# Batch 1's casts and copies reordered, H2's weight sums moved, and the last stores merged, in a linear-attention and gated-MLP kernel

## The chip, the cores and the metric

The kernel runs on one core of a Trainium2 chip. The metric is device time in microseconds (us) of one execution. A core has TensorE (PE, matrix products, with its weight loads shown as PEld), VectorE (DVE), ScalarE (ACT), GpSimd (POOL) and SyncE (SP). Each has its own instruction queue, worked through in order; between queues only semaphores set an order. DMAs are issued from the queues of SP, ACT and POOL and are carried out by 16 DMA engines.

## The reference

The inputs q, k and v are (8 batches, 8 heads, 576 positions, 64) in float32; w_in is 512x2048, w_out 2048x512, beta 2048.

```python
def phi(x): return np.where(x > 0, x, np.exp(x) - 1.0) + 1.0
q_p, k_p = phi(q), phi(k)
kv  = einsum('bhsd,bhse->bhde', k_p, v)
z   = k_p.sum(axis=2)
num = einsum('bhsd,bhde->bhse', q_p, kv)
den = einsum('bhsd,bhd->bhs', q_p, z)[..., None] + 1e-06
x   = (num / den), heads side by side: (4608 tokens, 512)
h   = x @ w_in
g   = h / (1 + exp(-beta * h))
out = g @ w_out                       # (4608, 512), float32
```

## The kernel before

**Tiling.** The work goes batch by batch. A batch has 576 positions, that is 64 groups (g) of 9 (j). Positions j = 0 to 7 make four token tiles of 128 rows, which are the batch's 512 columns in the MLP; the positions j = 8 of all eight batches are gathered in `xT_tail` and make a ninth block of 512 columns at the end (b = 8, called B in the code). The MLP of block b has an H phase (`h_phase`: 16 groups `ff` of four matmuls of 512 columns, L404, each followed by a silu on ACT, L412) and a Y phase (`y_phase` for blocks 0 and 1; `y_fast`, L755, for blocks 2 to 8, which saves products by sums and differences of g and of w_out, the latter prepared in `ws` by `w_sum`, L697). Below, H1 is the H phase of block 1, Y2 the Y phase of block 2, and so on.

**Overlap.** While TensorE works on the MLP of block b, the attention of batch b+1 is done between its groups: `kv_both` (L213; k^T v and, through a column of ones, z), then the numerators (`numer`, or `numer_all`, L319, from batch 2 on), the division on DVE into `xs_sb`, and the transpose into `xT`, on TensorE for batches 0 and 1 (`x_trans`, L381, with a copy by ACT or DVE), by DMA from batch 2 on. phi is an exp on ACT (`phi_exp`), a relu on DVE (`phi_relu`, L168) and a minimum on DVE (`phi_min`, L175). v arrives in float32 in the one buffer `vf` and is cast into `vaug` by POOL (`v_copy`, L203); only when both halves are cast may the next batch's v be loaded into `vf` (`load_v`).

**Order.** It is written out by hand (`manual_schedule`): each engine executes its instructions in the order in which the Python issues them. Up to L690 that is a straight list; afterwards `h_phase` and the Y phases call what `at(sh, ff, ...)` and `at(sy, n, ...)` hang behind a group or a product. The pool `hps` has four PSUM banks (`bank`), used in a ring by h, y and part of the numerators; `wps` has two pairs of banks (`banks`), used in a ring by `kv_both`, numerators and x transposes.

**Places that the change touches.** Batch 1's stretch is L627 to L690: MLP products `y_mm(0, t, i)` of block 0 (token tile t, quarter i of w_out) stand between `kv_both(1)`, `numer(1, t)` and `x_trans(1, t)`. `y_out` copies a finished y from PSUM with DVE and `y_store` sends it from SP. `w_out_scale(nc.scalar, 3)` scales quarter 3 of w_out on ACT. In `next_loads` (L842), called behind H's first group, POOL casts the next batch's v, waits by the tiny copy into `gate` for the transposed q of that batch (`qTd`) and then issues the loads of the batch after it. Two calls per store are due to `half(i)`: 64 partitions each. `g_diff` and `g_sums` (L716, L720) are DVE work on g behind groups 3, 7, 11 and 15 of an H phase.

Of the kernel before, what the change touches and what calls it, by code (L numbers as in the profile page):

```python
# [16 lines left out]
def kernel(  # L17
# [183 lines left out]
            phi_min(b, a, pr)  # L201

    def v_copy(eng, b, pr):  # L203
        eng.tensor_copy(  # L204
            vaug[b % 2][:, pr, :, :, 0:D],
            vf[:, 2 * pr : 2 * pr + 2].rearrange("p h j d -> p j h d"),
        )

    def half(hh):
        return slice(hh * G, (hh + 1) * G)  # L210
# [47 lines left out]
    def q_copy(eng, b, pr, tp):  # L258
        copy(eng, st[b, "qT"][:, pr, 0:4].rearrange("p t h n -> p (t h n)"), tp)
# [166 lines left out]
    def rows(b, ts):  # L426
# [2 lines left out]
            return out[b * S : (b + 1) * S, :].rearrange("(g j) m -> g j m", j=J)[:, ts]  # L429
        return out.rearrange("(b g j) m -> g b j m", b=B, j=J)[:, ts, J - 1]  # L430

    def y_store(b, t, c0=0, c1=512):
        for i in range(2):
            nc.sync.dma_start(
                out=rows(b, slice(2 * t + i, 2 * t + i + 1))[:, 0, c0:c1],
                in_=(y1, y2)[t % 2][half(i), (t // 2) % 2, c0:c1],
            )
# [6 lines left out]
    def w_out_scale(eng, i, cs=range(4)):  # L444
        for c in cs:
            ff = 4 * i + c
            if eng is nc.scalar:
                eng.mul(w_out_sb[i][:, c, :], w_out_f[i][:, c, :], rbeta[:, ff : ff + 1])
            else:
                eng.tensor_scalar(  # L450
                    w_out_sb[i][:, c, :], w_out_f[i][:, c, :], rbeta[:, ff : ff + 1],
                    1.0, ALU.mult, ALU.mult,
                )
# [6 lines left out]
    def load_v(b):  # L460
        if b < B:
            load(nc.gpsimd, vf, v, b)
# [169 lines left out]
            phi_relu(1, x, pr, xin(1, x, pr))  # L632
    phi_min(1, "q", 0)
    phi_min(1, "q", 1)
    for pr in range(2):
        v_copy(nc.gpsimd, 1, pr)
    load_v(2)
    for i in range(2):
        for t in range(4 - i):
            y_mm(0, t, i, yps[t])  # L640
# [4 lines left out]
    q_last(1, qtp[1][:, 1024 : 1024 + 2 * P])  # L645
    y_mm(0, 3, 1, yps[3])
    q_copy(nc.scalar, 1, 0, qtp[0][:, 0:1024])
    w_out_scale(nc.vector, 2)
    phi_min(1, "k", 0)
    phi_min(1, "k", 1)  # L650
    q_copy(nc.vector, 1, 1, qtp[1][:, 0:1024])
    q_copy_last(nc.vector, 1, qtp[1][:, 1024 : 1024 + 2 * P])
    w_out_scale(nc.scalar, 3)
    for t in range(3):
        y_mm(0, t, 2, yps[t])
    kv_both(1)
    phi_tile(2, "q")
    phi_tile(2, "k")
    y_mm(0, 3, 2, yps[3])
    numer(1, 0)  # L660
    y_mm(0, 0, 3, yps[0])
    numer(1, 1)
    x_trans(1, 0, nc.scalar)
    phi_exp(2, "q", 0, xin(2, "q", 0))
    y_mm(0, 1, 3, yps[1])
    numer(1, 2)
    y_out(0, 0, yps[0])
    x_trans(1, 1, nc.scalar)
    phi_exp(2, "q", 1, xin(2, "q", 1))
    y_mm(0, 2, 3, yps[2])  # L670
    numer(1, 3)
    y_out(0, 1, yps[1])
    x_trans(1, 2, nc.scalar)
    phi_exp(2, "k", 0, xin(2, "k", 0))
    y_mm(0, 3, 3, yps[3])
    x_trans(1, 3, nc.vector)
    phi_exp(2, "k", 1, xin(2, "k", 1))
    table(ACTF.Silu)
    y_out(0, 2, yps[2], store=False)
    y_out(0, 3, yps[3], store=False)  # L680
    numer_mm(1, 4)
    for pr in range(2):
        phi_relu(2, "q", pr, xin(2, "q", pr))
        phi_min(2, "q", pr)
    q_trans_dma(2)
    numer_xs(1, 4)
    x_trans_dma(1, 4)
    for t in range(2, 4):
# [36 lines left out]

    def h_phase(b, x, side):
        for ff in range(FC):
            hp = bank("h_ps")
            h_mm(x, ff, hp)
            silu(b, ff, hp)  # L730
            if b in FAST:
                if ff in (3, 7):
                    g_diff(b, slice(ff - 3, ff + 1))
                if ff in (11, 15):
                    g_sums(b, ff - 11, ff - 7)
            run(side, ff)
# [18 lines left out]
    def y_fast(b, side):  # L755

        g = g_sb[b % 2]
        pa, pd, pc, pb = [bank(n) for n in ("ya", "yd", "yc", "yb")]

        pbs = [banks("yb")[:, 0], banks("yb")[:, 0]] if b == B else [pb, pb]  # L760

        def part(n0, half2):
            def lhs(c, p):
                t0 = half2 * HM + p * P
                return g[:, n0 + c, t0 : t0 + P]
            return lhs

        def sums(n):
            return lambda c, p: gs[n][:, c, p * P : (p + 1) * P]

        def plain(n0, c0):
            return lambda c: w_out_sb[(n0 + c) // 4][:, (n0 + c) % 4, c0 : c0 + HM]

        def wsum(n):
            return lambda c: ws[n][:, c, :]

        def product(ps, lhs, rhs, first, ts=range(2), apart=False):
            for p in ts:
                for c in range(8):
                    nc.tensor.matmul(  # L780
                        ps[:, p * HM : (p + 1) * HM], lhs(c, p), rhs(c),
                        start=(first and (p == 0 or apart) and c == 0), stop=True,
                        skip_group_check=True,
                    )

        def v3(ps):
            return ps.rearrange("p (a m) -> p a m", a=2)

        r1 = work.tile([P, 512], F32, tag="r1", name="r1", bufs=1)
        u2 = work.tile([P, 512], F32, tag="u2", name="u2", bufs=1)  # L790
        u4 = work.tile([P, 512], F32, tag="u4", name="u4", bufs=1)
        u3 = work.tile([P, 512], F32, tag="u3", name="u3", bufs=1)
        if b < B - 2:
            table(ACTF.Exp)
        product(pa, part(0, 0), plain(0, 0), True)
        nc.scalar.copy(r1, pa)
        run(side, 0)
        product(pd, sums(2), wsum(2), True)
        run(side, 1)
        product(pa, part(8, 0), plain(8, 0), False)  # L800
        nc.scalar.copy(y1[:, :, 0:HM], v3(pa))
        run(side, 2)
        product(pc, sums(1), wsum(1), True)
        nc.vector.tensor_add(u2, pc, r1)  # L804
        nc.vector.tensor_add(u3, pd, u2)  # L805
        run(side, 3)
        if b == B:
            for i in range(2):
                nc.sync.dma_start(
                    out=rows(b, slice(i, i + 3, 2))[:, :, 0:HM], in_=y1[half(i), :, 0:HM]  # L810
                )
        for p in range(2):
            product(pbs[p], sums(0), wsum(0), True, (p,), b == B)
        for p in range(2) if b == B else ():
            ps = slice(p * HM, (p + 1) * HM)
            nc.vector.tensor_add(y2[:, p, HM:DM], pbs[p][:, ps], u3[:, ps])
        if b < B:
            nc.vector.tensor_add(y2[:, :, HM:DM], v3(pb), v3(u3))  # L818
        run(side, 4)
        product(pd, part(8, 1), wsum(3), False)  # L820
        nc.vector.tensor_add(y2[:, :, 0:HM], v3(pd), v3(u2))
        for i in range(2):
            nc.sync.dma_start(out=rows(b, slice(4 + i, 4 + i + 3, 2)), in_=y2[half(i)])
        run(side, 5)
        if b < B:
            product(pb, sums(3), plain(8, HM), False)
            nc.vector.tensor_add(y1[:, :, HM:DM], v3(pb), v3(u2))
            for i in range(2):
                nc.sync.dma_start(out=rows(b, slice(i, i + 3, 2)), in_=y1[half(i)])
        else:  # L830
            for p in range(2):
                ps = slice(p * HM, (p + 1) * HM)
                product(pbs[p], sums(3), plain(8, HM), False, (p,))
                nc.vector.tensor_add(y1[:, p, HM:DM], pbs[p][:, ps], u2[:, ps])  # L834
                for i, eng in enumerate((nc.sync, nc.scalar)):
                    eng.dma_start(
                        out=rows(b, slice(i + 2 * p, i + 2 * p + 1))[:, 0, HM:DM],
                        in_=y1[half(i), p, HM:DM],
                    )
        run(side, 6)  # L840

    def next_loads(b):  # L842
# [8 lines left out]
    for b in range(1, B + 1):  # L851
        n, m = b + 1, b + 2
        sh, sy = {}, {}
        if n < B:
            at(sh, 0, lambda: next_loads(n))
            at(sh, 8 if b == 1 else 1, lambda: kv_both(n))
            at(sh, 11 if b == 1 else 4, lambda: numer_all(n))
        if b in (1, 2) and FAST:
            for k_ in ((0, 2), (1, 3))[b - 1]:
                for n_ in range(2):  # L860
                    at(sh, 15 if b == 1 else k_, lambda k_=k_, n_=n_: w_sum(k_, n_))
        if m < B:
            y = (lambda a, f: f) if b in FAST else (lambda a, f: a)
            at(sy, 0, lambda: phi_tile(m, "q"), lambda: phi_part(m, "q", 0))
            at(sy, 1, lambda: phi_part(m, "q", 1))
            at(sy, 1, lambda: q_trans_dma(m))
            at(sy, y(6, 3), lambda: phi_tile(m, "k"), lambda: phi_part(m, "k", 0))
            at(sy, y(8, 4), lambda: phi_part(m, "k", 1), lambda: table(ACTF.Silu))
        h_phase(b, xT[b % 2] if b < B else xT_tail, sh)
        (y_fast if b in FAST else y_phase)(b, sy)  # L870
# [30 lines left out]
```

## Time and profile before

| | us |
|---|---|
| median of 3 runs | 282.42 |
| the runs | 280.89, 282.42, 282.59 |
| profiled execution | 280.67 |
| its span | 278.9 |
| TensorE busy in the span | 267.2 (96%) |
| DVE busy | 169.2 (61%) |
| ACT busy | 169.1 (61%) |
| POOL busy | 46.3 (17%) |

The span runs from the first to the last instruction in the trace; the execution's own time has some 1.8 us around it. The stretches of the span: batch 0's attention up to about 21 us, H0 to 32, Y0 with batch 1's attention to 51.6, H1 to 67, Y1 to 81, H2 to 97, Y2 to 109.7, and then some 28 us for each further block; the last product ends at 273.7. A line of a timeline gives the start (us), the busy time, engine, source line, operation, output and inputs with sizes, and in brackets the idle time of the engine before it and what ended it. A busy matmul includes its way through the pipeline: matmuls that follow one another are nearer in their starts than their busy time. DMA calls appear under SPq, ACTq or POOLq with the time their issue takes.

### The profile page before, as it was taken

The page shows a single profiled execution, that of the slowest core. Times are in us where ns is not written, and L with a number is a line of the kernel's source. Part 1 is how long each engine was busy: PE and PEld are TensorE (multiplying, and loading weights), DVE is VectorE, ACT ScalarE, POOL GpSimd, SP SyncE. Part 2 cuts the span into 40 slices and gives each one's busy share as a digit, 9 for nine tenths or more (in the row PEclk, how much of TensorE's full clock was granted, in tenths as well). Part 3 has the DMA queues.
Part 4 walks back from the last instruction along what each step waited for, and adds up shares of the span by engine and source line. Part 5 has one row for each costly group of instructions (what it writes and reads, how often), then busy time and mean ns, then how long its engine had stood idle before and what let it go on. Part 6 is the DMA issues. An engine that isn't in the chain of part 4 may idle for free.

```text
span 278.9 us, 6374 instructions
## 1 busy us (share of the span) xinstructions
PE 267.2 (96%) x2689; PEld 167.0 (60%) x2697; DVE 169.2 (61%) x329; ACT 169.1 (61%) x231; POOL 46.3 (17%) x60
## 2 busy tenths in 40 slices
PE   6799999999999999999999999999999999999992
PEld 2475455445444487548754875487548745864681
DVE  4772485958848797568757885788572414321532
ACT  4838876975925794579457945794572076127500
POOL 5923012303043030304030303030000000000000
PEclk9999999999999999999999999999999999999998
DMA  7999999559999946994799659956430130041014
GB/s 237 248 207 351 268 373 264 142 94 180 289 150 182 300 65 101 205 293 66 105 198 284 79 97 204 280 83 98 142 75 12 35 118 0 0 101 52 0 40 113
DMA packets 49292, 42.76 MB, mean 153 GB/s; under 512 B 30816, under 2 KB 41072, under 8 KB 49264
## 3 DMA queue, kind: packets, MB, share of 16 engines
q0 software_dynamic: 13040, 23.40, 36.0%
q1 hardware_dynamic: 36032, 18.82, 33.1%
q8 instruction: 21, 0.34, 0.5%
q10 hardware_dynamic: 192, 0.14, 0.2%
q14 instruction: 7, 0.06, 0.1%
HBM read 36.71 MB, written 9.44 MB: 165 GB/s over the span
## 4 chain that ended last, share of the span: by engine, by line
PE 59%; DVE 2%; issue 0%; DVEq 0%
PE h_ps L404 30%; PE yb L780 8%; PE yd L780 8%; PE ya L780 8%; PE yc L780 4%; PE kvp L223 1%; PE nps L331 1%; DVE phi_q L175 1%; DVE r L168 0%; DVE u L804 0%; DVE y L818 0%; DVE u L805 0%; DVE y L834 0%; DVE phi_k L175 0%; DVEq L818 0%
## 5 line engine op out<-in xcount | busy, mean ns | idle before, releaser
L412 ACT ACTIVATE g<-h_ps,beta_c 128x512 bf16<-128x512 f32 x144 | 97.8, 688 | 68.7 <-PE h_ps L404 68.7
L404 PE MATMUL h_ps<-xT,w_in 128*128 128x512 bf16 (+1 forms) x560 | 114.8, 361 | 0.4 <-DVE xT L241 0.2
L404 PEld LDWEIGHTS <-w_in 128*128 128x128 bf16 x624 | 57.3, 98 | 63.1 <-DVE xs_sb L346 1.1
L780 PEld LDWEIGHTS <-stage 128*128 128x128 bf16 x448 | 43.8, 98 | 5.5 <-issue 0.4
L780 PEld LDWEIGHTS <-g 128*128 128x128 bf16 x336 | 32.9, 98 | 5.4
L204 POOL CAST vaug<-vf 128x1152 bf16<-128x1152 f32 x14 | 18.8, 1372 | 83.8 <-DMA vf<-in_v_dram 83.8
L419 PE MATMUL y_ps<-w_out,g 128*128 128x512 bf16 x123 | 28.7, 379 | 0.4 <-issue 0.2
L780 PE MATMUL ya<-w_out,g 128*128 128x256 bf16 x224 | 26.7, 273 | 0.0
L718 DVE TENSOR_TENSOR stage<-g 128x1024 bf16<-128x1024 bf16 x14 | 9.6, 685 | 21.6 <-ACT g L412 21.6
L722 DVE TENSOR_TENSOR stage<-g 128x1024 bf16<-128x1024 bf16 x14 | 9.7, 692 | 20.7 <-ACT g L412 20.7
L346 DVE TENSOR_TENSOR xs_sb<-nps,rden 128x448 bf16<-128x448 f32 (+3 forms) x30 | 20.7, 689 | 1.0
L419 PEld LDWEIGHTS <-g 128*128 128x128 bf16 x128 | 12.2, 98 | 13.7
L163 ACT ACTIVATE e<-xk 128x1152 bf16<-128x1152 bf16 (+1 forms) x15 | 16.7, 1160 | 0.3 <-DMA xk<-in_k_dram 0.2
L163 ACT ACTIVATE e<-xq 128x1152 bf16<-128x1152 bf16 x14 | 15.6, 1159 | 0.0
L175 DVE TENSOR_TENSOR phi_q<-e,r 128x1152 bf16<-128x1152 bf16 x16 | 12.9, 805 | 2.9 <-ACT e L163 1.8
L156 ACT ACT_TABLE_LOAD x11 | 14.1, 1283 | 0.2
L404 PE MATMUL h_ps<-xT_tail,w_in 128*128 128x512 bf16 x62 | 13.9, 379 | 0.1
L175 DVE TENSOR_TENSOR phi_k<-e,r 128x1152 bf16<-128x1152 bf16 x16 | 12.8, 804 | 1.7 <-DVE r L168 0.5
L780 PE MATMUL yb<-w_out,stage 128*128 128x256 bf16 x112 | 13.4, 272 | 0.2 <-DVE y L818 0.2
L780 PE MATMUL yd<-ws,stage 128*128 128x256 bf16 x112 | 13.4, 273 | 0.0
L780 PE MATMUL yb<-ws,stage 128*128 128x256 bf16 x112 | 13.4, 273 | 0.0
L724 DVE TENSOR_TENSOR stage<-g,stage 128x1024 bf16<-128x1024 bf16 x14 | 13.1, 934 | 0.5
(96 smaller groups left out, 232.1 us busy)
## 6 DMA issues: line engine op xcount, KB each, us to landing
vf<-in_v_dram POOLq DMA_DIRECT2D x7, 1152.0 KB, 13.5
out_dram<-y SPq DMA_DIRECT2D x26, 256.0 KB, 3.7
xq<-in_q_dram POOLq DMA_DIRECT2D x7, 576.0 KB, 8.4
xk<-in_k_dram POOLq DMA_DIRECT2D x7, 576.0 KB, 11.4
out_dram<-y SPq DMA_DIRECT2D x18, 128.0 KB, 3.2
w_in<-in_moe_w_in_dram POOLq DMA_DIRECT2D x4, 512.0 KB, 11.5
g<-in_moe_w_out_dram POOLq DMA_DIRECT2D x2, 1024.0 KB, 17.0
stage<-in_moe_w_out_dram POOLq DMA_DIRECT2D x2, 1024.0 KB, 21.4
```

Of the source, the lines that this page charges most:

```text
L156: nc.scalar.activation(act0, warm[:, 0:1], func)
L163: nc.scalar.activation(e, x, ACTF.Exp)
L175: nc.vector.tensor_tensor(st[b, a][:, pr].rearrange("p j (h d) -> p j h d", h=2), st[b, a, pr, "e"].rearrange("p h j d -> p j h d"), st[b, ...
L204: eng.tensor_copy(vaug[b % 2][:, pr, :, :, 0:D], vf[:, 2 * pr : 2 * pr + 2].rearrange("p h j d -> p j h d"),)
L346: nc.vector.tensor_mul(xs_sb[:n, ils, v0 * D : v1 * D].rearrange("p i (u d) -> p i u d", d=D), pv[:, :, :, 0:D], rden[:, :, :, None].to_br ...
L404: nc.tensor.matmul(hp[:, c0:c1].rearrange("p (t n) -> p t n", n=P), w_in_sb[ff // 4][:, kc, (ff % 4) * P : (ff % 4 + 1) * P], xm, start=(k ...
L412: nc.scalar.activation(g_sb[b % 2][:, ff, :], hp, ACTF.Silu, scale=beta_c[:, ff : ff + 1])
L419: nc.tensor.matmul(yp[:, c0:c1], g_sb[b % 2][:, ff, t * P : (t + 1) * P], w_out_sb[i][:, c, c0:c1], start=(ff == 0), stop=(ff == FC - 1), ...
L718: nc.vector.tensor_sub(gs[2][:, c], g[:, c, 0:HM], g[:, c, HM:512])
L722: nc.vector.tensor_add(gs[0][:, c], g[:, c, HM:512], g[:, c2, HM:512])
L724: nc.vector.tensor_sub(gs[3][:, c], g[:, c2, 0:HM], gs[1][:, c])
L780: nc.tensor.matmul(ps[:, p * HM : (p + 1) * HM], lhs(c, p), rhs(c), start=(first and (p == 0 or apart) and c == 0), stop=True, skip_group_ ...
```

## The change

Six edits:

1. Batch 1's v is cast half by ACT, half by POOL, later in the list (behind batch 1's first q copy); `load_v(2)` follows it.
2. The products of block 0 are shifted among batch 1's attention steps: two instead of three quarter-2 tiles ahead of `kv_both(1)`, and the last product behind the last x transpose. The copies `y_out(0, 0)` and `y_out(0, 1)` stand behind more of the numerators and x transposes.
3. In H1 the groups 4 and 5 take their two banks from the pairs' pool; `kv_both(2)` and `numer_all(2)` are called one group later.
4. A tiny POOL copy that reads batch 2's phi(q) is put ahead of POOL's casts of batch 2's v.
5. In H2 the sums `ws[1]` and `ws[3]` are made behind groups 7 and 8 instead of 1 and 3.
6. The stores of block 8 use one call for 128 partitions (`tail_rows`) where two calls for 64 stood, four calls in place of eight; of the two for y1's second half the first is issued by ACT and the second by SP, where each of SP and ACT had issued half of either.

```diff
     def v_copy(eng, b, pr):
-        eng.tensor_copy(
-            vaug[b % 2][:, pr, :, :, 0:D],
+        copy(
+            eng, vaug[b % 2][:, pr, :, :, 0:D],
             vf[:, 2 * pr : 2 * pr + 2].rearrange("p h j d -> p j h d"),
         )
...
+    def tail_rows(p, n=1):
+
+        r = out.rearrange("(p n j) m -> n p j m", n=P, j=J)
+        return r[:, p : p + n, J - 1]
...
     phi_min(1, "q", 1)
-    for pr in range(2):
-        v_copy(nc.gpsimd, 1, pr)
-    load_v(2)
...
     q_copy(nc.scalar, 1, 0, qtp[0][:, 0:1024])
+    v_copy(nc.scalar, 1, 0)
+    v_copy(nc.gpsimd, 1, 1)
+    load_v(2)
     w_out_scale(nc.vector, 2)
...
-    for t in range(3):
+    for t in range(2):
         y_mm(0, t, 2, yps[t])
     kv_both(1)
     phi_tile(2, "q")
     phi_tile(2, "k")
+    y_mm(0, 2, 2, yps[2])
+    numer(1, 0)
     y_mm(0, 3, 2, yps[3])
-    numer(1, 0)
-    y_mm(0, 0, 3, yps[0])
     numer(1, 1)
     x_trans(1, 0, nc.scalar)
     phi_exp(2, "q", 0, xin(2, "q", 0))
-    y_mm(0, 1, 3, yps[1])
+    y_mm(0, 0, 3, yps[0])
     numer(1, 2)
-    y_out(0, 0, yps[0])
     x_trans(1, 1, nc.scalar)
     phi_exp(2, "q", 1, xin(2, "q", 1))
+    y_mm(0, 1, 3, yps[1])
+    numer(1, 3)
+    x_trans(1, 2, nc.scalar)
+    y_out(0, 0, yps[0])
+    phi_exp(2, "k", 0, xin(2, "k", 0))
     y_mm(0, 2, 3, yps[2])
-    numer(1, 3)
-    y_out(0, 1, yps[1])
-    x_trans(1, 2, nc.scalar)
-    phi_exp(2, "k", 0, xin(2, "k", 0))
-    y_mm(0, 3, 3, yps[3])
     x_trans(1, 3, nc.vector)
     phi_exp(2, "k", 1, xin(2, "k", 1))
     table(ACTF.Silu)
+    y_out(0, 1, yps[1])
+    y_mm(0, 3, 3, yps[3])
     y_out(0, 2, yps[2], store=False)
...
     q_trans_dma(2)
+    nc.gpsimd.tensor_copy(gate, st[2, "q"][:, 1, J - 1, P - 1 : P])
     numer_xs(1, 4)
...
         for ff in range(FC):
-            hp = bank("h_ps")
-            h_mm(x, ff, hp)
+            if b == 1 and ff in (4, 5):
+
+                if ff == 4:
+                    pair = banks("h_ps")
+                    for i in range(2):
+                        h_mm(x, ff + i, pair[:, i])
+                hp = pair[:, ff - 4]
+            else:
+                hp = bank("h_ps")
+                h_mm(x, ff, hp)
             silu(b, ff, hp)
...
         if b == B:
-            for i in range(2):
-                nc.sync.dma_start(
-                    out=rows(b, slice(i, i + 3, 2))[:, :, 0:HM], in_=y1[half(i), :, 0:HM]
-                )
+            nc.sync.dma_start(out=tail_rows(0, 2)[:, :, 0:HM], in_=y1[:, :, 0:HM])
...
-        for i in range(2):
+        if b == B:
+            nc.sync.dma_start(out=tail_rows(2, 2), in_=y2)
+        for i in range(2) if b < B else ():
             nc.sync.dma_start(out=rows(b, slice(4 + i, 4 + i + 3, 2)), in_=y2[half(i)])
...
-                for i, eng in enumerate((nc.sync, nc.scalar)):
-                    eng.dma_start(
-                        out=rows(b, slice(i + 2 * p, i + 2 * p + 1))[:, 0, HM:DM],
-                        in_=y1[half(i), p, HM:DM],
-                    )
+                (nc.scalar, nc.sync)[p].dma_start(
+                    out=tail_rows(p)[:, 0, HM:DM], in_=y1[:, p, HM:DM]
+                )
...
-            at(sh, 8 if b == 1 else 1, lambda: kv_both(n))
-            at(sh, 11 if b == 1 else 4, lambda: numer_all(n))
+            at(sh, 9 if b == 1 else 1, lambda: kv_both(n))
+            at(sh, 12 if b == 1 else 4, lambda: numer_all(n))
...
-                    at(sh, 15 if b == 1 else k_, lambda k_=k_, n_=n_: w_sum(k_, n_))
+                    at(sh, 15 if b == 1 else 7 + k_ // 2, lambda k_=k_, n_=n_: w_sum(k_, n_))
```

## The prediction

> **What bounds the kernel now.** I read the slices first, then the chain that ended last, then the timeline where TensorE is not continuous. From the page (section 2: busy tenths in 40 slices of 7 us; section 4: the chain):
>
> ```profile
> span 278.9 us, 6374 instructions
> ...
> PE   6799999999999999999999999999999999999992
> ...
> PEclk9999999999999999999999999999999999999998
> ...
> PE 59%; DVE 2%; issue 0%; DVEq 0%
> PE h_ps L404 30%; PE yb L780 8%; PE yd L780 8%; PE ya L780 8%; PE yc L780 4%; PE kvp L223 1%; PE nps L331 1%; DVE phi_q L175 1%; DVE r L168 0%; DVE u L804 0%; DVE y L818 0%; DVE u L805 0%; DVE y L834 0%; DVE phi_k L175 0%; DVEq L818 0%
> ```
>
> The chain is matmuls, at full granted clock, so a matmul of 512 columns costs its pitch: 36 of L404 take 7.93 us in H1, the last a full 0.38, so (7.93-0.38)/35 = 0.216, four in 0.863. No edit removes a matmul. The change can only close gaps between matmuls and shorten what follows the last one. So I set the timeline's matmul starts against this pitch (a gap of exactly one pitch is a missing record). Real gaps are in four places: some 1.6 us at 42 to 52 us (batch 1's attention), 0.4 at 89 (H2), 0.37 at 107.6 (Y2), and 5.2 behind the last product (273.7 to 278.9).
>
> **Batch 1 (42 to 52 us).** From the timeline (start, busy, then the idle time before and who ended it):
>
> ```profile
> 40.58 2.24 POOL L204 CAST vaug<-vf 128x1152 bf16<-128x1152 f32 x2 [12.60 <-DMA vf<-in_v_dram]
> 42.85 0.80 PE L223 MATMUL kvp<-vaug,phi_k 64*64 64x65 bf16 x72
> 43.78 0.87 DVE L235 CAST kv_bd<-kvp 64x260 bf16<-64x260 f32 x2 [2.43 <-PE kvp L223]
> 44.71 0.41 PE L298 MATMUL nps<-kv_bd,qT 128*128 128x130 bf16 x4
> 44.96 1.20 PE L419 MATMUL y_ps<-w_out,g 128*128 128x512 bf16 x4
> 50.69 0.23 PEld L386 LDWEIGHTS <-xs_sb 128*128 128x128 bf16 x4 [0.75 <-DVE xs_sb L311]
> 51.62 7.93 PE L404 MATMUL h_ps<-xT,w_in 128*128 128x512 bf16 x36 [0.18 <-DVE xT L241]
> 52.68 0.45 DVE L168 TENSOR_SCALAR r<-xq 128x1152 bf16<-128x1152 bf16 x1
> 53.23 1.51 DVE L175 TENSOR_TENSOR phi_q<-e,r 128x1152 bf16<-128x1152 bf16 x1
> 55.21 0.76 DVE L175 TENSOR_TENSOR phi_q<-e,r 128x1152 bf16<-128x1152 bf16 x1
> ```
>
> The two POOL casts end at 42.82 and kv_both(1) starts at 42.85: the cast sets it. The last x transpose waits for DVE (0.75), which copied y ahead of xs; H1 waits for xT (0.18); the first product with w_out quarter 3 takes 1.20, not the 1.03 of its neighbours, because ACT is still scaling that quarter (43.17 + 2.56 = 45.73).
>
> v lands at 40.58, which no edit moves. Now POOL casts one half (2.24/2 = 1.12) and ACT the other. ACT is free from 40.0 (its q copy) to 43.17 (w_out quarter 3's landing), so nothing behind the cast is late. No row shows ACT writing this strided tile; its exp of 1152 elements takes 1.17, DVE's copy of 1024 into qT 0.68 and POOL's pair 2.24. I take 1.16 (same engine, same size); 0.68 to 2.24 bounds it.
>
> I walk the new order with rows. Twelve y matmuls from 39.30 end at 41.89. Casts end 41.74. kvp starts at 41.99 (0.1 for the change of shape, as at 42.75 to 42.85). The casts to kv_bd start 0.93 later and take 0.87, so the first numer is at 43.85, against 44.71. From a numer's start to xs it is 0.45 + 1.13 (den 45.16 to xs end 46.28), 0.06 more to the transpose. Numer, numer, transpose then follow at 43.85, 44.93, 45.49; the last transpose at 49.85 instead of 50.69, a y group behind it (0.863, which now hides xT's copy), numer 4, and H1 at 51.2. The same walk over the old order gives 51.86 where 51.62 was measured, so it errs by 0.24. The gain by it is 0.66; I take **0.6**, bounds -0.2 (ACT's cast 2.24: the walk then gives H1 at 52.06) and +1.0 (all waits there but the changes of shape).
>
> What then comes late in H1: silu starts after the exps and the table load, 53.98 before and 53.2 by the walk. Four banks last 51.2 + 3.45 = 54.65, so silu holds nobody even without the two banks more; I cost them at nothing, their cover being 0.8 us. kv_both(2), one group later, is asked for at 51.2 + 10 x 0.863 + 0.1 = 59.9. It needs phi_k and batch 2's v. v's cast now waits behind phi(q) (54.9 by the walk): gate 0.2, two casts under contention 2.6 (2.48 there, 2.96 at 76.58), done 57.9. The 0.75 that phi(q) loses to the cast (1.51 against 0.76) is gone, and up to 2 x 0.75 comes to phi(k) instead: 59.1. Cover 0.8. On POOL the next loads queue behind the casts, but they waited for qTd at 62.36 anyway. numer_all(2) is asked for at 63.4 and its qTd comes about 1 us earlier than 62.3. H2's xT landed at 79.7 for a start at 81.08, so it has 1.3.
>
> The Trainium skill (GPSIMD Engine Reference, Specifications) says that POOL contends with DVE instructions in a 2-port perf mode or with two SBUF inputs, which speaks against laying the cast on phi(k). The rows agree for the tensor_tensor (1.51), not for the relu, which took 0.45 inside the cast at 52.68. With both relus doubled phi_k would end at 60.0 and cost 0.1; by the row nothing.
>
> Moving the y copies and stores (y_store(0,0) and (0,1)) later costs nothing: the banks of y 0 to 3 are wanted by H1's groups 0 to 3, from 51.2 to 53.8, and are copied out by 52.5 by the walk; SP's transposes of batch 2 wait for phi(q), not for these stores.
>
> **H2's sums.** From the timeline:
>
> ```profile
> 86.33 0.88 PE L331 MATMUL nps<-kv_q,qTd 64*64 64x65 bf16 x72
> 86.90 1.28 DVE L706 TENSOR_TENSOR ws<-w_out,ws 128x1024 bf16<-128x1024 bf16 x2
> 88.11 0.16 DVE L344 TENSOR_SCALAR den<-nps 128x7 f32<-128x7 f32 x1
> 89.21 0.55 PEld L404 LDWEIGHTS <-w_in 128*128 128x128 bf16 x4 [0.66 <-DVE xs_sb L346]
> ```
>
> numer_all's first bank is evacuated from 88.11, behind g_diff and a w_sum; two groups later TensorE wants that bank and waits. Eight matmuls from 87.14 end at 88.87, the next is at 89.21: 0.34, and the second bank adds 0.09 at 90.1. Without the sum DVE starts at g_diff's end, 86.98, 1.1 earlier, so both go: **0.4** (0.0 to 0.43). The four sums (2.5 us) now follow the evacuation. DVE idles there 0.61 at 94.56 and 1.24 at 98.01, and the 1.1 is free too: 92.2 evacuated, g_diff to 92.8, sums to 95.3, first g_sums to 97.4. The second g_sums are released by silu at 97.56. They just fit, by 0.15.
>
> **Y2's 0.37** (yb starts at 107.94 behind DVE's y at 107.20; its forerunner ended at 107.57) comes from DVE being 0.2 late at u2 and 0.4 of unexplained idle before phi_k. v(4)'s cast now meets a different piece of DVE's work; 0 to 0.37, I take **0.15**.
>
> **The tail.**
>
> ```profile
> 272.69 1.25 SPq L823 DMA_DIRECT2D out_dram<-y  x2
> 273.31 1.35 ACTq L836 DMA_DIRECT2D out_dram<-y  x2
> 273.72 0.42 DVE L834 TENSOR_TENSOR y<-yb,u 128x256 f32<-128x256 f32 x1 [0.45 <-PE yb L780]
> 274.03 2.02 SPq L836 DMA_DIRECT2D out_dram<-y  x2
> ```
>
> SP issues four stores back to back; the last leaves at 275.01 though its data is ready at 274.15. With one call for y2 (0.6) and one for the last piece it leaves at 274.2: 0.8 sooner. But the 16 DMA engines are 89% busy from 273.9 to 277.3 with these same bytes (packet times sum to 49.3 us, /16 = 3.08 of 3.45), so full engines give only 0.37. A call of 128 partitions on this path to memory has no row; SP's loads of 128 partitions took 0.49 to issue, the half stores 0.6, and twice 0.6 with the first packet 0.6 late is the other end. Bounds -0.6 to +0.8; I take **0.35**. The merged y1 store at 267.4 is off the path.
>
> **Sum:** 0.6 + 0.4 + 0.15 + 0.35 = 1.5. The profiled execution took 280.67 (span 278.9 and 1.8 around it), so 279.2 in its like. It agrees with the fastest run (280.89); the median is 282.42. Taking 1.5 off the median: **280.9**. Within 1% (2.8 us) is about what a measurement of this kernel can tell from no change.
>
> **Rivals.**
> - *All closes* (0.2): batch 1 gives 1.0, H2 0.43, Y2 0.37, the tail 0.8: 2.6, 279.8. For it: every gap named has its wait; against: the DMA engines' 89%.
> - *The cast does not split* (0.15): ACT needs 2.24 for its half, and kvp stays at 42.85; batch 1 gives -0.2, the sum is 0.7, 281.7. Against: ACT's 1.17 rows.
> - *DVE overflows in Y2* (0.12; slower): place, the second g_sums. It decides when DVE is more than the 0.15 late behind silu 15. If the evacuation does not start earlier, the sums push the first g_sums to 96.5 to 98.7 and the second into v(4)'s cast (from 98.5), where all three tensor_tensors take 1.51 (4.5, against 3.7 of before): they end at 103.2, not 101.8, the four phi(q) steps (2.5) then bring u2 to 105.8, not 104.28, and yb waits 1.5 longer. H2's 0.4 and Y2's 0.15 are gone too: 0.6 + 0.35 - 1.5 = 0.55 slower, 283.0. For it: the thin 0.15; against: DVE has nothing else at 86.98.
> - *Forecast*: 0.53.
>
> **Range.** From the first rival, and 0.8 less because the before runs themselves lie 1.7 apart, to the last rival: 279.0 to 282.9. Faster by over 1% needs 2.8 us, the first rival with a quick set of runs: 0.16. Slower by over 1% needs the overflow and a bad tail: 0.05.
>
> **What the changed profile would show.** ACT casting at 40.6 for about 1.2 beside one POOL cast; kvp near 42.0; H1 near 51.0 and silu from 53.2; POOL's next casts from about 55.3, with phi_k (not phi_q) at 1.51; kv_both(2) without a wait; no wait of L404 for xs_sb in H2; the last SP store issued about 0.1 after DVE's last y. Wrong would be: an ACT cast near 2 us, a wait of kvp for phi_k in H1, DVE behind at u2, or a tail still 5.2 long.

## The result, and the profile after

| | before | changed |
|---|---|---|
| median, runs taken for the prediction and right after it (4 and 4) | 281.95 us | 277.77 us |
| ratio, 95% interval | | 0.9865 (0.9822 to 0.9908) |
| profiled execution, span | 280.67, 278.9 us | 277.78, 276.0 us |
| median, later on one chip (27 and 6) | 280.82 us | 278.63 us |
| ratio, 95% interval | | 0.9929 (0.9906 to 0.9951) |

The changed kernel is faster, by about 1%: by 4.2 us against the few runs of the first row, by 2.2 against the many of the later one, by 2.9 between the two profiled spans. The kernel before was run 59 times more in three groups, with medians of 280.82, 280.64 and 280.93. The 282.42 that the prediction started from was a median of three that happened to lie high.

Where the 2.9 us of the span went, read from the starts of the same matmuls in both traces (us):

| | before | changed | gained by then |
|---|---|---|---|
| first product after batch 1's q transposes | 39.30 | 38.87 | 0.43 |
| v of batch 1 landed (16th part of its DMA) | 40.52 | 40.60 | |
| `kv_both(1)` | 42.85 | 41.83 | 1.02 |
| H1 | 51.62 | 51.09 | 0.53 |
| H2 | 81.08 | 80.49 | 0.59 |
| Y2 | 97.09 | 96.06 | 1.03 |
| H3 | 109.68 | 108.31 | 1.37 |
| last product | 271.77 | 270.30 | 1.47 |
| end | 278.89 | 276.01 | 2.88 |

The first row precedes every edit: that execution ran 0.43 earlier from batch 0 on, and waiting for v swallowed at least 0.26 of it again; up to 0.17 of batch 1's 0.53 is from there and not from the edits (see `batch1_only`). So between these two traces batch 1 gave 0.53, H2 0.44, Y2 0.34, and the stretch behind the last product's start 1.41 (7.12 to 5.71); 0.16 lie in between. From the page of the changed kernel (span, slices, chain by engine):

```profile
span 276.0 us, 6367 instructions
...
PE   7899999999999999999999999999999999999994
...
PEclk9999999999999999999999999999999999999999
...
PE 82%; DMA 13%; DVE 1%; POOL 1%; issue 1%; ACT 0%; DVEq 0%; POOLq 0%
```

The chain is unbroken now (before, it began at 102 us, with DVE's work in Y2): it runs back to 51 us through TensorE alone, but for 0.05 us here and there, and ahead of that through batch 1 to v's DMA. Batch 1 in the timeline of the changed kernel (start, busy, in brackets the idle time before and who ended it):

```profile
40.62 1.15 ACT L239 CAST vaug<-vf 128x1152 bf16<-128x1152 f32 x1 [1.06 <-DMA vf<-in_v_dram]
40.66 1.15 POOL L241 CAST vaug<-vf 128x1152 bf16<-128x1152 f32 x1 [12.58 <-DMA vf<-in_v_dram]
41.83 0.80 PE L223 MATMUL kvp<-vaug,phi_k 64*64 64x65 bf16 x72 [0.21 <-ACT vaug L239]
43.69 0.41 PE L298 MATMUL nps<-kv_bd,qT 128*128 128x130 bf16 x4
49.55 0.23 PEld L386 LDWEIGHTS <-xs_sb 128*128 128x128 bf16 x4 [0.63 <-DVE xs_sb L311]
51.09 8.81 PE L404 MATMUL h_ps<-xT,w_in 128*128 128x512 bf16 x40
52.68 0.76 DVE L175 TENSOR_TENSOR phi_q<-e,r 128x1152 bf16<-128x1152 bf16 x1
54.87 2.46 POOL L241 CAST vaug<-vf 128x1152 bf16<-128x1152 f32 x2
56.43 1.50 DVE L175 TENSOR_TENSOR phi_k<-e,r 128x1152 bf16<-128x1152 bf16 x1
59.83 0.80 PE L223 MATMUL kvp<-vaug,phi_k 64*64 64x65 bf16 x72
```

The two casts run side by side, each 1.15; TensorE waits 0.21 for ACT's. The last x transpose still waits for xs_sb (0.63), H1 no longer for xT. phi(q) is down to 0.76, one phi(k) up to 1.50, and `kv_both(2)` at 59.83 waits for neither. In H2 (the same timeline), den follows g_diff and no wait for xs_sb is left:

```profile
85.70 0.69 DVE L725 TENSOR_TENSOR stage<-g 128x1024 bf16<-128x1024 bf16 x1 [1.97 <-ACT g L412]
86.31 0.16 DVE L344 TENSOR_SCALAR den<-nps 128x7 f32<-128x7 f32 x1
86.56 3.63 PE L404 MATMUL h_ps<-xT,w_in 128*128 128x512 bf16 x16
```

In Y2 the products follow one another as ya, yd, ya, yc, yb, yd, yb, named by their PSUM banks; u is DVE's sum of yc and r, y its sum of yb and u, and the last yb may not start before that y is read. Y2 before, DVE's rows ahead of that y:

```profile
105.61 0.45 DVE L168 TENSOR_SCALAR r<-xk 128x1152 bf16<-128x1152 bf16 x1
106.53 0.76 DVE L175 TENSOR_TENSOR phi_k<-e,r 128x1152 bf16<-128x1152 bf16 x1 [0.46 <-DVE r L168]
107.20 0.68 DVE L818 TENSOR_TENSOR y<-yb,u 128x512 f32<-128x512 f32 x1
```

Changed:

```profile
104.60 0.45 DVE L168 TENSOR_SCALAR r<-xk 128x1152 bf16<-128x1152 bf16 x1
105.15 0.76 DVE L175 TENSOR_TENSOR phi_k<-e,r 128x1152 bf16<-128x1152 bf16 x1
105.83 0.68 DVE L830 TENSOR_TENSOR y<-yb,u 128x512 f32<-128x512 f32 x1
```

The idle time ahead of phi_k is gone, and with it the 0.37 for which TensorE waited ahead of the last yb.

And the tail: y2 in one call, one call by ACT, one by SP, which leaves 0.03 behind DVE's last y (272.25 + 0.42):

```profile
271.23 0.38 SPq L835 DMA_DIRECT2D out_dram<-y  x1
271.84 0.37 ACTq L849 DMA_DIRECT2D out_dram<-y  x1
272.25 0.42 DVE L848 TENSOR_TENSOR y<-yb,u 128x256 f32<-128x256 f32 x1 [0.45 <-PE yb L795]
272.70 0.34 SPq L849 DMA_DIRECT2D out_dram<-y  x1
```

The last landing fell from 6.1 us behind the last product's start to 4.4 (277.85 to 274.73). That is more than the 0.8 by which the last call is earlier. The windows of both traces show why: stretches of 1.3 us from y2's first packets on, columns window, length, busy time of PE, PEld, DVE, ACT, POOL, granted clock, share of the DMA engines, GB/s.

Before:

```profile
273.90:275.20 1.30, 0.00 (x0) 0.00 (x0) 0.24 (x1) 0.00 (x0) 0.00 (x0) 1.00 0.97 194
```

Changed:

```profile
272.10:273.40 1.30, 0.12 (x2) 0.00 (x0) 0.42 (x1) 0.00 (x0) 0.00 (x0) 1.00 1.00 372
```

The DMA engines are full in both, and carry nearly twice as much: a packet of 2 KB took 141 ns in the mean before and 88 after. From y2's first packet to the last packet of all it is 3.36 us before (273.94 to 277.30) and 2.21 after (272.12 to 274.33), so 1.15 of the gain lies there; the first packet is 0.36 earlier behind the last product's start.

### The profile page after: what moved, and what is told of

It is laid out like the page before. It is cut to its first block, busy times and chain, and to the rows that moved or that the text cites. A ratio compares the mean times of both kernels' runs of the same rounds, so it can differ in the third digit from the quotient of the medians.

```text
span 276.0 us, 6367 instructions
## 1 busy us (share of the span) xinstructions
PE 267.8 (97%) x2688; PEld 167.6 (61%) x2697; DVE 169.7 (61%) x329; ACT 170.1 (62%) x232; POOL 45.6 (17%) x60
## 2 busy tenths in 40 slices
DMA packets 49228, 42.76 MB, mean 155 GB/s; under 512 B 30752, under 2 KB 41008, under 8 KB 49200
## 4 chain that ended last, share of the span: by engine, by line
PE 82%; DMA 13%; DVE 1%; POOL 1%; issue 1%; ACT 0%; DVEq 0%; POOLq 0%
PE h_ps L404 41%; PE yb L795 9%; PE ya L795 9%; PE yd L795 9%; DMA vf<-in_v_dram 8%; PE y_ps L419 6%; PE yc L795 4%; DMA w_in<-in_moe_w_in_dram 4%; PE kvp L223 2%; PE nps L331 2%; DMA stage<-in_q_dram 1%; POOL vf L100 1%; PE nps L298 1%; DVE xs_sb L311 1%; ACT vaug L239 0%
## 5 line engine op out<-in xcount | busy, mean ns | idle before, releaser
L175 DVE TENSOR_TENSOR phi_k<-e,r 128x1152 bf16<-128x1152 bf16 x16 | 13.5, 850 | 1.4
L795 PE MATMUL yc<-ws,stage 128*128 128x256 bf16 x112 | 13.4, 273 | 0.0
L795 PE MATMUL yd<-ws,g 128*128 128x256 bf16 x112 | 13.4, 273 | 0.0
```

The lines of the kernel that those rows point to most:

```text
L175: nc.vector.tensor_tensor(st[b, a][:, pr].rearrange("p j (h d) -> p j h d", h=2), st[b, a, pr, "e"].rearrange("p h j d -> p j h d"), st[b, ...
L795: nc.tensor.matmul(ps[:, p * HM : (p + 1) * HM], lhs(c, p), rhs(c), start=(first and (p == 0 or apart) and c == 0), stop=True, skip_group_ ...
```

## The experiments

Times are medians, with the kernel before run beside them on the same chip. "Tail" is the time from the last product's start to the end, "gap ahead of yb" TensorE's idle time ahead of Y2's last product. The runs of one set and the medians of two sets differ by some tenths of a microsecond, so single gaps are read from the traces.

**One part at a time.** Four kernels beside 27 runs of the kernel before (280.82 us).

`tail_only`: the kernel before with edit 6.

```diff
+            nc.sync.dma_start(out=tail_rows(0, 2)[:, :, 0:HM], in_=y1[:, :, 0:HM])
...
+            nc.sync.dma_start(out=tail_rows(2, 2), in_=y2)
...
+                (nc.scalar, nc.sync)[p].dma_start(
+                    out=tail_rows(p)[:, 0, HM:DM], in_=y1[:, p, HM:DM]
+                )
```

> The kernel before with edit 6 alone (block 8's stores in four calls of 128 partitions). Theory 1, the partitions that a call spans set how fast its packets move: the 2 KB packets of y2 take about 88 ns in the mean, as in the changed kernel, not 141, and the time behind the last product's start falls from 7.1 to 5.7 us, 1.4 less in all. Rival, only the later issue of the last store was the cost and the DMA engines are as full as before: packets stay near 141 ns and 0.4 to 0.8 us are gained.

Measured: 279.75 us, ratio 0.9967 (0.9950 to 0.9984); tail 5.70, packets of 2 KB 88 ns. These are theory 1's numbers, in the trace; the median gives 1.1 of the 1.4.

`batch1_only`: the changed kernel with edits 5 and 6 undone.

```diff
-            at(sh, 15 if b == 1 else 7 + k_ // 2, lambda k_=k_, n_=n_: w_sum(k_, n_))
+            at(sh, 15 if b == 1 else k_, lambda k_=k_, n_=n_: w_sum(k_, n_))
```

(and the old stores)

> The changed kernel with the old w_sum places and the old stores, so edits 1 to 4 alone. Theory: H1 starts 0.5 us earlier for the same landing of v, and 0.5 to 0.6 us are gained in all; the waits in H2 (0.43) and behind the last product (7.1 us) stay. Rival: batch 1's edits also take away the 1.7 us by which some executions of the kernel before are longer, then the median falls by 1.5 us or more and its runs lie close together.

Measured: 280.06 us, ratio 0.9974 (0.9964 to 0.9984), 0.76 gained. H1 starts 10.49 us behind v's landing (51.19 to 40.70); in five kernels with the old order this is 10.96 to 11.10. Seven kernels with the new order have the 10.49. Three variants of the changed kernel below have 10.82, 11.11 and 11.84 (`y2_halves`, `y2_rows`, `y2_early`): there TensorE's own products come last, and H1 starts 11.95 to 11.96 behind the first product after the q transposes, where the old order needs 12.32 (the kernel before and `before_plus1`). So batch 1's edits give 0.5 where the loads come last (10.49 for 10.96 to 10.98) and 0.36 where TensorE's products do. At the first product of the kernel before, 39.30, the new order would thus have reached H1 at 51.26 (an estimate, 39.30 + 11.96), not 51.09. H2's wait (0.34 and 0.09) and the tail (7.10) are as before. The gap ahead of yb is gone, which I had put down to neither; with its 0.37 the 0.76 leaves 0.39 for batch 1. The rival falls: of 27 runs of the kernel before one alone (282.59) is longer by 1.7 us or more.

`sums_only`: the kernel before with edit 5.

```diff
-            at(sh, 15 if b == 1 else k_, lambda k_=k_, n_=n_: w_sum(k_, n_))
+            at(sh, 15 if b == 1 else 7 + k_ // 2, lambda k_=k_, n_=n_: w_sum(k_, n_))
```

> The kernel before with edit 5 alone (ws[1] and ws[3] behind groups 7 and 8 of H2). Theory: the wait of L404 for xs_sb in H2 goes, 0.43 us; Y2's gap of 0.37 us ahead of the last yb product goes with it if it came from DVE's order in H2, total 0.8; it stays if it came from where v's cast meets DVE, total 0.4. Rival of the forecast: the second g_sums are pushed back and yb waits 1.5 us longer, 0.5 to 1 us slower.

Measured: 280.32 us, ratio 0.9983 (0.9967 to 1.0000). H2's wait is gone, but in Y2 TensorE now idles 0.31 (ahead of yd) and 0.46 (ahead of yb), against 0.37 before. By the trace the two cancel, 0.43 less and 0.40 more. The median says 0.50 less, with an interval that reaches 0, so the time settles neither of the totals expected; the slowdown of the rival did not come. The second g_sums are not pushed back: they start 0.92 behind Y2's start, as before. The timeline of DVE in this kernel shows what is late:

```profile
99.41 0.46 DVE L168 TENSOR_SCALAR r<-xq 128x1152 bf16<-128x1152 bf16 x1
100.40 0.76 DVE L175 TENSOR_TENSOR phi_q<-e,r 128x1152 bf16<-128x1152 bf16 x1 [0.54 <-ACT e L163]
101.07 1.40 DVE L168 TENSOR_SCALAR r<-xq 128x1152 bf16<-128x1152 bf16 x1
102.58 1.51 DVE L175 TENSOR_TENSOR phi_q<-e,r 128x1152 bf16<-128x1152 bf16 x1
104.01 0.68 DVE L804 TENSOR_TENSOR u<-yc,r 128x512 f32<-128x512 f32 x1
105.33 0.45 DVE L168 TENSOR_SCALAR r<-xk 128x1152 bf16<-128x1152 bf16 x1
106.26 0.76 DVE L175 TENSOR_TENSOR phi_k<-e,r 128x1152 bf16<-128x1152 bf16 x1 [0.48 <-ACT act L156]
```

v(4)'s cast (from 100.41 here) now meets the second half of phi(q), right ahead of u, so u is late and yd waits 0.31. And there is 0.48 of idle ahead of phi_k that no product and no cast explains.

`after_again`: the changed kernel, on the same chip.

> The changed kernel itself, beside its parts on one chip. If the parts add, its gain is the sum of the three others' (by the two profiles 1.4 + 0.5 + 0.8 = 2.7 us of the span, while the medians say 4.2). If the medians' 4.2 repeats and the parts' sum does not reach it, the edits act together.

Measured: 278.63 us, ratio 0.9929 (0.9906 to 0.9951), 2.2 gained. The three parts alone give 1.07 + 0.76 + 0.50 = 2.3. The 4.2 does not repeat. That the parts add up is agreement within intervals of some 0.3 to 0.6 us each, no more: the 0.50 is not in `sums_only`'s trace, and 0.37 of the 0.76 is Y2's.

**What makes the tail faster.** Four variants of y2's last store in the changed kernel, beside 18 runs of the kernel before (280.64 us).

```diff
-            nc.sync.dma_start(out=tail_rows(2, 2), in_=y2)
+            for i in range(2):                                    # y2_halves
+                nc.sync.dma_start(out=tail_rows(2, 2)[half(i)], in_=y2[half(i)])
+            for i in range(2):                                    # y2_evenodd
+                nc.sync.dma_start(out=tail_rows(2, 2)[i::2], in_=y2[i::2])
+            for i in range(2):                                    # y2_rows
+                nc.sync.dma_start(out=tail_rows(2 + i)[:, 0], in_=y2[:, i])
```

> The changed kernel with y2's last store cut again into partitions 0 to 63 and 64 to 127, two calls on SP. Theory 1 (a call whose partitions all lie in one half of the 128 moves its packets slowly): the first 128 packets of 2 KB take about 150 to 160 ns as before the change, the mean is 120 to 140, and 0.7 to 1.2 us of the tail's 1.4 are lost. Rival 1 (the rate does not hang on the partitions): 88 ns and no more than 0.3 us lost for the second call's issue.

> The changed kernel with y2's last store cut into even and odd partitions, again two calls of 64 partitions, 128 packets each. Theory 1, it is the half of the partition range that matters, not the count of 64: packets near 88 ns and the tail within 0.3 us of the changed kernel's 5.7. Rival 2, a call of 64 partitions is slow whichever they are: packets near 140 ns and the tail as with the two halves.

> The changed kernel with y2's last store cut by token, two calls of 128 partitions and 128 packets each. Theory 1 and rival 2: packets near 88 ns, tail within 0.3 us of 5.7. Rival 3, the number of packets per call sets the pace: near 140 ns.

Measured:

| y2's last store | packets of 2 KB, mean | tail | median |
|---|---|---|---|
| one call, 128 partitions (changed kernel) | 88 ns | 5.70 | |
| `y2_halves` | 141 (first 128: 187, second 128: 96) | 7.02 | 279.66 |
| `y2_evenodd` | 88 | 6.08 | 278.68 |
| `y2_rows` | 88 | 5.63 | 278.44 |

The first 1.3 us of y2's packets, windows as above. Two halves:

```profile
273.10:274.40 1.30, 0.00 (x0) 0.00 (x0) 0.21 (x1) 0.00 (x0) 0.00 (x0) 1.00 1.00 186
```

Even and odd partitions:

```profile
273.20:274.50 1.30, 0.00 (x0) 0.00 (x0) 0.14 (x1) 0.00 (x0) 0.00 (x0) 1.00 1.01 361
```

Neither the number of calls nor that of partitions or packets per call sets the rate: 64 partitions spread over the whole range go at 361 GB/s, partitions 0 to 63 at 186. Rivals 1, 2 and 3 fall. Of theory 1 only one half holds: the second call, for partitions 64 to 127, is not slow (96 ns). The stores of blocks 2 to 7, cut into the same halves in both kernels, agree: their first 128 packets take 143 to 168 ns, the second 104 to 113. A pair of calls of the kernel before, its first 1.3 us and then the second call's packets:

```profile
138.90:140.20 1.30, 1.30 (x75) 0.86 (x73) 0.00 (x0) 1.12 (x2) 0.51 (x2) 1.00 0.95 187
140.45:141.10 0.65, 0.65 (x4) 0.29 (x3) 0.38 (x1) 0.00 (x0) 0.65 (x2) 1.00 0.97 303
```

So the slow call is the one for partitions 0 to 63. It is also always the first of the two; no run stores 64 to 127 first, so whether it is these partitions, or that of two half calls the first is slow, stays open, as does the reason.

A smaller part is issue time: a call of 64 partitions takes SP 0.6 to 0.65 us where no other holds it up, one of 128 0.33 to 0.42; the last of several takes longer (1.04 in the kernel before, 0.47 in `y2_evenodd`, 1.22 in `y2_halves`). With even and odd y2's first packet moves 1.30 us after its call began (271.89 to 273.19), in `y2_rows` 0.84 (272.09 to 272.93), and the tail is 0.4 longer, though the last call leaves equally early.

`y2_early`: the right half of y2's columns is stored when it is there, ahead of the last two products.

```diff
             nc.vector.tensor_add(y2[:, p, HM:DM], pbs[p][:, ps], u3[:, ps])
+        if b == B:
+            nc.sync.dma_start(out=tail_rows(2, 2)[:, :, HM:DM], in_=y2[:, :, HM:DM])
...
-            nc.sync.dma_start(out=tail_rows(2, 2), in_=y2)
+            nc.sync.dma_start(out=tail_rows(2, 2)[:, :, 0:HM], in_=y2[:, :, 0:HM])
```

> The changed kernel with the right half of y2's columns stored as soon as it is there (one product and a half before the end) and only its left half behind the product before the last. Theory: 256 KB leave the busy stretch at the end, in which the 16 engines are full for 2.2 us; the last store's packets start when they are issued (0.9 us behind the issue) instead of behind y2's, and the tail falls from 5.7 to 5.2 us. Rival, the last store's own issue, packets and completion are the floor already: the tail stays at 5.6 to 5.7.

Measured: tail 5.34, 0.36 of the expected 0.5. The median, 278.69 (0.9924, 0.9896 to 0.9952), does not show it: in its profiled execution the first product after batch 1's q transposes is at 40.33, in the others at 38.9 to 39.6, and its runs spread from 277.6 to 280.6.

**Batch 1 and Y2.** Four kernels beside 14 runs of the kernel before (280.93 us).

`pool_casts`: the changed kernel with both casts on POOL.

```diff
-    v_copy(nc.scalar, 1, 0)
+    v_copy(nc.gpsimd, 1, 0)
     v_copy(nc.gpsimd, 1, 1)
```

> The changed kernel with both halves of batch 1's v cast by POOL again, all else as changed. Theory: the split cast is what batch 1's edits live on. kv_both(1) starts 2.25 to 2.3 us after v's landing instead of 1.2, and H1 follows 1.0 us later than in the changed kernel, 11.5 after the landing instead of 10.5: slower than the kernel before in this stretch (11.0), since two tiles of y instead of three stand ahead of kv_both. Rival, the reordering of x ahead of the y copies is what pays: H1 stays within 0.3 of 10.5.

Measured: 278.90 us, ratio 0.9931 (0.9915 to 0.9948). H1 starts 11.28 behind v's landing, 0.8 later than in the changed kernel and 0.2 to 0.3 later than with the old order. Without the split the new order loses, so batch 1's gain needs it. In this order the split is worth 0.8, not 1.0, because kv_both starts on the half that is ready:

```profile
40.83 2.24 POOL L241 CAST vaug<-vf 128x1152 bf16<-128x1152 f32 x2 [12.62 <-DMA vf<-in_v_dram]
42.15 0.48 PE L223 MATMUL kvp<-vaug,phi_k 64*64 64x65 bf16 x36
43.13 0.48 PE L223 MATMUL kvp<-vaug,phi_k 64*64 64x65 bf16 x36 [0.50 <-POOL vaug L241]
```

Where the old order lost its time is another matter. In its five traces `kv_both(1)` starts 3.54 to 3.55 behind the first product, when the sixteen products ahead of it are through, and it takes 0.80 to 1.00, so it waits inside by 0.2 at most. What else is waited for there is ACT's scaling of quarter 3 of w_out (0.20 to 0.24 of idle time ahead of that product's last matmul in `tail_only`, `sums_only` and `sums_gatek`; 1.20 for 1.03 in the kernel before) and xT (0.18). The new order puts quarter 3's products later and hides xT's copy behind a product; it also calls `kv_both` a tile earlier, and that pays only with the split. The split in the old order was not run.

`h1_old`: the changed kernel without edits 3 and 4.

```diff
-            if b == 1 and ff in (4, 5):
+            if b == B + 9 and ff in (4, 5):
...
-            at(sh, 9 if b == 1 else 1, lambda: kv_both(n))
-            at(sh, 12 if b == 1 else 4, lambda: numer_all(n))
+            at(sh, 8 if b == 1 else 1, lambda: kv_both(n))
+            at(sh, 11 if b == 1 else 4, lambda: numer_all(n))
...
-    nc.gpsimd.tensor_copy(gate, st[2, "q"][:, 1, J - 1, P - 1 : P])
```

> The changed kernel without the two banks more in H1, with kv_both(2) and numer_all(2) behind groups 8 and 11 again, and without the gate ahead of POOL's casts of batch 2's v (edits 3 and 4 undone). Forecast, these three are worth nothing by themselves: phi(q) takes 1.5 us once instead of phi(k), kv_both(2) waits for phi_k by 0.2 to 0.3 us, no more, and the time is within 0.3 us of the changed kernel's. Rival, they hold the gain of H1: silu or phi_k holds TensorE and 0.6 us or more are lost.

Measured: 279.08 us, ratio 0.9936 (0.9912 to 0.9959). Four banks hold nobody up (36 matmuls in 7.94 us), and kv_both(2) stops inside for 0.2 until phi_k is there. That much was expected. But the gap ahead of yb is back, 0.38, so the forecast that these edits are worth nothing missed: by the traces they hold 0.2 in H1 and this gap.

`sums_gatek`: `sums_only` with v(4)'s cast kept behind phi(k)'s first half.

```diff
     def next_loads(b):
+        if b == 4:
+            nc.gpsimd.tensor_copy(gate, st[b, "k"][:, 0, J - 1, P - 1 : P])
         for pr in range(2):
             v_copy(nc.gpsimd, b, pr)
```

> The kernel before with edit 5 and, in H2/Y2 alone, a tiny POOL copy that reads the first half of batch 4's phi(k), ahead of POOL's casts of batch 4's v, so that these can't meet DVE's g_sums and phi(q). Theory: Y2's gap ahead of the last yb product (0.78 us with edit 5 alone, 0.37 before) comes from v's cast slowing DVE ahead of u2; it falls to 0.1 or less. Rival, DVE has too much to do there whatever POOL does, or the 0.4 idle ahead of phi_k is of another cause: 0.4 or more stay.

Measured: 280.88 us, ratio 1.0003 (0.9985 to 1.0021); gap ahead of yb 0.37, and none ahead of yd. The median does not show the 0.44 by which H2 is shorter in its trace (81.26 to 96.83; before 81.08 to 97.09); its runs spread from 280.0 to 282.2. My theory was half right. With the cast out of the way DVE does phi(q) at full speed and waits for yc at u. What stays is the idle time ahead of phi_k:

```profile
104.02 0.69 DVE L804 TENSOR_TENSOR u<-yc,r 128x512 f32<-128x512 f32 x1 [1.22 <-PE yc L780]
105.35 0.45 DVE L168 TENSOR_SCALAR r<-xk 128x1152 bf16<-128x1152 bf16 x1
106.27 0.76 DVE L175 TENSOR_TENSOR phi_k<-e,r 128x1152 bf16<-128x1152 bf16 x1 [0.47 <-DVE r L168]
```

Over all traces by then, this idle time stood in the five in which that phi_k has 191 instructions ahead of it in DVE's list (419 in all, waits included) and in none of the nine in which it has 190 (418 in all). The numbers 190 to 192 below count in this way, from 0. Edits 3 and 4 together take one instruction off DVE's list ahead of it.

`after_plus1` and `before_plus1`: the two kernels with one idle instruction more on DVE, far ahead, and nothing else.

```diff
     nc.vector.memset(ones, 1.0)
+    spare = consts.tile([P, 1], BF16, name="spare")
+    nc.vector.memset(spare, 1.0)
```

> The changed kernel with one tiny memset more on DVE, in its first 3 us, that nobody reads. Theory: the 0.4 us that DVE idles ahead of batch 4's first phi(k) in Y2 belongs to the place in DVE's list: it is there in every kernel in which this instruction is DVE's 191st in the trace and in none in which it is the 190th. With the memset it is the 191st again: the idle time of 0.4 and the gap of 0.35 to 0.5 ahead of the last yb product come back. Rival, the idle comes from what the edits do in H1 or with v's cast: then the gap stays at 0.2 or less.

> The kernel before with the same memset; batch 4's first phi(k) becomes the 192nd. Theory: the idle of 0.4 ahead of it goes or moves to another instruction, and the gap ahead of the last yb product falls from 0.37 to 0.2 or less. Rival: 0.37 stays.

Measured, one run each (278.46 and 280.08 us): in the changed kernel the instruction has number 191 again, and the idle time and a gap of 0.45 ahead of yb are back; in the kernel before it has 192, and the gap is gone altogether. DVE's timelines, changed kernel plus one:

```profile
105.01 0.45 DVE L170 TENSOR_SCALAR r<-xk 128x1152 bf16<-128x1152 bf16 x1
105.92 0.76 DVE L177 TENSOR_TENSOR phi_k<-e,r 128x1152 bf16<-128x1152 bf16 x1 [0.46 <-ACT act L158]
```

Kernel before plus one:

```profile
105.59 0.45 DVE L170 TENSOR_SCALAR r<-xk 128x1152 bf16<-128x1152 bf16 x1
106.14 0.76 DVE L177 TENSOR_TENSOR phi_k<-e,r 128x1152 bf16<-128x1152 bf16 x1
```

So the idle time belongs to the place in DVE's list: with v's cast, H1 and all else as they were, one instruction more brings it in the one kernel and takes it away in the other. Why this place has it (the fetching of the list is the obvious guess) no run here shows. The 0.31 ahead of yd in the first of the two is v(4)'s cast on phi(q) again (from 4.27 behind Y2's start, as at 3.99 in `sums_only`). `y2_halves`, `y2_rows` and `y2_early`, whose Y2 is the changed kernel's, have it too (0.31, the cast from 4.0 to 4.3 behind Y2's start): it hangs on when v(4) lands, so the changed kernel does not save Y2's 0.34 in every execution.

`best`: the changed kernel with `y2_early` and the gate of `sums_gatek`.

> The changed kernel with two more edits: y2's right half of the columns stored early (tail 5.3 instead of 5.7 us) and the same tiny POOL copy ahead of the casts of batch 4's v (Y2's gap 0.0 to 0.2 in the changed kernel, here 0). If both hold, 0.4 to 0.6 us below the changed kernel, some 278.1 where that has 278.6; if not, the same as the changed kernel.

Measured: 277.28 us (277.15 to 277.40), ratio 0.9867 (0.9852 to 0.9881): below the changed kernel, whose interval in its own set begins at 0.9906. In the trace both edits do what they should: tail 5.33, no gap in Y2. That is 0.4 to 0.6 us; the medians of two sets lie 1.35 apart (278.63 and 277.28), and what the rest is, four and six runs can't tell.

## Why the prediction was wrong

It forecast 280.9 us in 279.0 to 282.9, 1.5 less than before; measured were 277.77, below the range, and gains of 2.2 to 4.2 (the 4.2 against four runs that lay high). By its steps:

- **The starting point** failed first: "Taking 1.5 off the median". The profiled execution (280.67) and the quickest run agreed, two of three runs lay 1.6 above, and 59 later runs put the kernel at 280.6 to 280.9. The forecast on the profile's own time, 279.2, missed the changed kernel's 277.78 by 1.4, the other by 3.1. Of that 1.4 the tail is 1.06 (1.41 for 0.35) and Y2 0.19.
- **The tail** is the mis-sized term: 0.35 forecast, 1.4 measured. The failing step is "full engines give only 0.37": it took the packets' times as given and asked only how full the engines were. They were full because each packet took 141 ns, and `tail_only` brought that to 88; `y2_halves` shows that a call for partitions 0 to 63 alone moves at half the rate. The trace of before held the hint: 256 KB at 194 GB/s with the engines at 97%, while the page has slices of loads at 373. The bound of +0.8 came from the issue alone and was too low for the same reason.
- **Batch 1**: 0.6 forecast, 0.53 between the two traces, 0.36 to 0.5 by all of them. "The cast sets it" was half of it: sixteen products from 39.30, at 0.216 each, end at 42.76, and with the 0.1 for the change of shape they too set 42.85. The walk moves a tile of y behind `kv_both` as well, so its sum did not suffer. ACT's cast took 1.15 for 1.16. From the new order the walk gave 51.2 for H1, and it is 51.09. The covers held: kv_both(2), asked for at 59.83 (59.9), found phi_k done at 59.2 (59.1) and the cast at 57.3 (57.9), and edits 3 and 4 cost nothing in H1; `h1_old` shows that they save 0.2 there, which the prediction put at nothing.
- **H2's sums**: 0.4 forecast, 0.44 measured, and DVE did fit. The rival of an overflow did not come.
- **Y2**: 0.15 forecast, 0.34 measured, for a reason that I did not have. I put the gap on v(4)'s cast meeting DVE. That is real and costs 0.3 to 0.4 where it meets phi(q), but the 0.37 of before was idle time at one place in DVE's list, removed because another edit shortened this list by one.
- **The relu** was read from a row that misled. At 52.68 it took 0.45 beside POOL's casts; that one began at the change from the first cast to the second. Elsewhere a relu beside a cast takes up to 1.40, as in the changed kernel's Y2:

```profile
98.44 1.51 DVE L731 TENSOR_TENSOR stage<-g,stage 128x1024 bf16<-128x1024 bf16 x1
99.88 1.40 DVE L168 TENSOR_SCALAR r<-xq 128x1152 bf16<-128x1152 bf16 x1
```

The Trainium skill (GPSIMD Engine Reference, Specifications) names two cases in which POOL and DVE contend, instructions with two SBUF inputs and those in a 2-port mode. The traces agree with the first (phi's minimum, 1.51 for 0.76); the relu's 1.40 would fit the second, but no run shows in which mode a relu runs. It cost nothing, since the cover in H1 held.

Of the rivals, "all closes" (2.6) came nearest, from another sum: more tail, less of batch 1.

## What to carry to other kernels

A DMA engine that is busy all the time is not at its rate: divide the bytes by the time and compare with other rows before calling it a floor. Let a store that ends on the critical path span the whole range of partitions; here two calls by columns or rows were as good as one, two calls by partition halves cost 1.3 us. Before blaming a neighbour for a short unexplained idle time, add one idle instruction far ahead: if the gap goes, or one comes, it is the place in the list. And before crediting one edit with a gap, see what else ended at the same time: the cast and the products ahead of `kv_both(1)` did.

## What the runs showed of the hardware that I had not expected

- Stores to memory from partitions 0 to 63 alone ran at 186 to 194 GB/s with all 16 DMA engines busy, from 64 partitions spread over the range at 361, from 128 at 362 to 372. The calls for 64 to 127 that followed were not slow: 303 GB/s in the pair shown.
- Issuing a store of 64 partitions from SP took about 0.6 us, one of 128 partitions 0.33 to 0.42, though it is larger; behind other calls 1.04 and 1.22 were seen.
- One place in DVE's list has 0.4 us of idle time in all six kernels in which a phi(k) stands there and in none of the other ten, and one memset more or less, 100 us earlier, decides on 0.4 us.
